# A fused retention and squared-ReLU kernel: the first weight block issued ahead of the first cast of v, fewer warm-up matmuls, and new written-out orders for every engine

## The chip, the cores and the metric

The kernel runs on one core of one Trainium2 chip. The metric is the device time of one execution in microseconds (us). The kernel before takes 283.64 us, the median of three runs (283.6, 283.64 and 287.75).

A core has five engines that run side by side, each through its own list of instructions in order: PE (matmuls; its weight loads are listed as PEld), DVE (vector), ACT (scalar), POOL (GpSimd) and SP (which here only issues DMA transfers). POOL issues transfers too: those that convert float32 to float16 on the way. The transfers themselves run on 16 DMA engines.

## The reference

With eight sequences, eight heads, 576 positions and head size 64, a retention layer feeds a two-layer network with a squared ReLU:

```python
scores = scale * np.matmul(q, k.transpose(0, 1, 3, 2))
rel = pos[:, None] - pos[None, :]
Dmat = np.where(rel >= 0, gamma[:, None, None] ** rel[None, :, :], 0.0)
ret = scores * Dmat[None, :, :, :]
attn_out = np.matmul(ret, v)
...
x = np.ascontiguousarray(attn_out.transpose(0, 2, 1, 3)).reshape(B * S, H * D)
h = x @ w_in
r = np.maximum(h, 0.0)
g = r * r
return g @ w_out
```

x has 4608 rows of 512, w_in is 512 x 2048 and w_out is 2048 x 512, all in float32. The kernel computes in float16 with float32 sums.

## The kernel before

**Tiling.** The positions are cut into 36 units of 128 rows: four full chunks for each of the eight sequences, and four "tail" units that hold the last 64 rows of two sequences each. Two units make a group; there are 18 groups. A group goes through two stages. The retention stage makes xT (the rows x, transposed) out of q, k and v and a running state R. The feed-forward stage multiplies xT with w_in, applies ReLU and square (gT), and multiplies gT with w_out.

**Retention.** The first eight units are loaded in pairs (add_load_pair, L441 and L444). Their k, q and v are cast on DVE, ACT and POOL to float16 (kx and qx at L555 and L553; vx, with a decay, at L548, one half on POOL and one half on DVE), transposed on PE (psT, L570) and copied out of PSUM as kqT (L587). Then come small matmuls, all issued by the helper quad at L483: psc (scores), psS (sums for the state), psO (outputs). DVE masks the scores (rx, L624), updates the state (stmp at L646, R at L597) and makes xT out of psO (L711). Later units are loaded one by one (L419, L422; tails L425), cast on POOL (kq at L497, L512, L508; v at L518) and transposed by DMA (kqT, L529); ACT copies their psO to xT (L887).

**Feed-forward.** The first product writes ph (L1207, or in seven-product Strassen form L1056), ACT and DVE take ReLU and square (L1217, L1224, L1226, L1085, L1099), and the second product writes po (L1246 for the first group, L1302 in Strassen form behind it). The sums that Strassen's form needs are made on DVE (stage, L1275; wT, L982; pair_c, L1020; xs, L1041). Results go to o (L1318, L1328, L1379, L1254) and are stored by SP (L999, and L1004 for the tails).

**Weights.** w_in and w_out come in eight blocks, numbered 0 to 7, each issued by POOL (L459) as a converting transfer. The first one is made to wait for the load of v of the first pair (the call of behind in add_weight). SP's load of k for the pair that starts at unit 4 waits for weight block 5 in the same way.

**The order of the work.** Nothing is scheduled while the program is built. A class Schedule holds 1848 tasks (1844 after the change) with their dependences; the list ORDER, written out by hand from a search, gives the one order in which all tasks of all engines are emitted, so it fixes the order on each engine. SLOTS gives, tag by tag, which buffer each tile takes: "ff" is the rotation of the eight PSUM banks. Tasks of the engine SP stand in ORDER with the rest, so SP's queue of loads, transposes and stores is fixed too. A store that waits for its tile holds up what is queued behind it on SP.

**Warm-ups and fillers.** WARM matmuls on zeros (L392) stand in the lead-in, before PE has real work. Empty PE instructions ("fillers") are set in two ways. FRONT of them are dealt out behind the warm-ups, some per warm-up. PADS gives, for each long run of small matmuls, how many are spread over the larger matmuls ahead of that run. They change at which instruction each run begins.

Of the kernel before, what the change touches and what calls it, by code (L numbers as in the profile page):

```python
# [73 lines left out]

SLOTS = {
    "ff": (
        "012345671235467210354216503216504123250356270617026170243671023026307156423105305315031472632140160724075325461034607134"
        "572614356746243562751420753140517345151076245010176145026157032173652056417016752657421360274072301673461053045206106214"
        "754067342671274302567325642076217067065460215722452361726434230"),
    "kq16": "012345610624530164204563014253601245306124503162",  # L80
# [1369 lines left out]
```

## Time and profile before

| what | us |
|---|---|
| median of three runs | 283.64 |
| own time of the profiled execution | 285.19 |
| span of the profiled execution, first to last instruction | 283.3 |
| PE busy | 273.1 |
| DVE busy | 202.5 |
| ACT busy | 197.2 |
| POOL busy | 100.7 |

The profile comes from one execution. Its own time is 1.9 us more than its span, which leaves out what lies before the first and behind the last instruction. Matmuls are pipelined, so that a busy PE is not a PE at its peak. The granted clock of PE is 1.000 over the whole span.

A row of the timeline gives start, duration, engine, line, operation, the tiles written and read, shapes and count; in brackets stands how long the engine was idle before it and what ended that wait. A row of the table of waits gives who waited for what, the sum in us, the number of times, and the longest. A row of the chain gives start, duration and what ran; the chain is followed backwards from the last instruction to whatever released each step. A row of the table by stretches gives the stretch, its length, each engine's busy time, the clock, the busy share of the DMA engines and their GB/s.

### The profile page before, as it was taken

The page shows a single profiled execution, that of the slowest core. Times are in us where ns is not written, and L with a number is a line of the kernel's source. Part 1 is how long each engine was busy: PE and PEld are TensorE (multiplying, and loading weights), DVE is VectorE, ACT ScalarE, POOL GpSimd, SP SyncE. Part 2 cuts the span into 40 slices and gives each one's busy share as a digit, 9 for nine tenths or more (in the row PEclk, how much of TensorE's full clock was granted, in tenths as well). Part 3 has the DMA queues.
Part 4 walks back from the last instruction along what each step waited for, and adds up shares of the span by engine and source line. Part 5 has one row for each costly group of instructions (what it writes and reads, how often), then busy time and mean ns, then how long its engine had stood idle before and what let it go on. Part 6 is the DMA issues. An engine that isn't in the chain of part 4 may idle for free.

```text
span 283.3 us, 11597 instructions
## 1 busy us (share of the span) xinstructions
PE 273.1 (96%) x4730; PEld 236.8 (84%) x4730; DVE 202.5 (71%) x405; ACT 197.2 (70%) x374; POOL 100.7 (36%) x133
## 2 busy tenths in 40 slices
PE   8799999999999999999999999999999989999994
PEld 3477677888899889989998998899879878999883
DVE  4781588989788958567887877767786866574562
ACT  6647786576759865996779568767688665787931
POOL 7650034714533743516256124444454230000000
PEclk9999999999999999999999999999999999999999
DMA  6999998889599999989799798897979890104014
GB/s 207 277 206 207 246 325 198 182 207 203 135 188 206 226 214 183 203 188 190 172 213 209 148 194 186 189 186 198 174 179 217 211 139 5 39 1 187 2 74 148
DMA packets 119154, 50.03 MB, mean 177 GB/s; under 512 B 94784, under 2 KB 113728, under 8 KB 119104
## 3 DMA queue, kind: packets, MB, share of 16 engines
q1 hardware_dynamic: 114560, 44.84, 73.4%
q0 software_dynamic: 4224, 4.19, 9.1%
q8 instruction: 39, 0.64, 1.0%
q10 hardware_dynamic: 320, 0.26, 0.4%
q14 instruction: 11, 0.09, 0.1%
HBM read 36.70 MB, written 9.44 MB: 163 GB/s over the span
## 4 chain that ended last, share of the span: by engine, by line
PE 78%; DMA 11%; ACT 2%; SPq 2%; POOL 2%; DVE 1%; issue 1%; POOLq 0%; DVEq 0%
PE po L1302 33%; PE ph L1207 22%; PE ph L1056 16%; PE psO L483 4%; DMA w_in<-in_moe_w_in_dram 4%; DMA loads<-in_v_dram 2%; DMA pair_c<-in_v_dram 2%; DMA loads<-in_q_dram 2%; DMA kqT<-kq 1%; SPq L425 1%; PE psS L483 1%; PE psc L483 1%; ACT gT L1224 1%; POOL vx L548 1%; SPq L441 1%
## 5 line engine op out<-in xcount | busy, mean ns | idle before, releaser
L1207 PE MATMUL ph<-xT,w_in 128*128 128x256 f16 x640 | 84.0, 273 | 1.2 <-issue 0.6
L1207 PEld LDWEIGHTS <-w_in 128*128 128x128 f16 x640 | 61.4, 98 | 11.3 <-issue 1.5
L1217 ACT ACTIVATE gT<-ph 128x512 f16<-128x512 f32 x80 | 46.1, 599 | 18.6 <-PE ph L1207 18.5
L1302 PEld LDWEIGHTS <-gT 128*128 128x128 f16 x544 | 51.0, 98 | 6.8 <-issue 0.4
L1302 PE MATMUL po<-w_out,gT 128*128 128x256 f16 x272 | 45.8, 273 | 0.0
L1302 PE MATMUL po<-wT,stage 128*128 128x256 f16 x272 | 42.3, 273 | 0.6 <-ACT xT L887 0.6
L1302 PEld LDWEIGHTS <-stage 128*128 128x128 f16 x408 | 38.2, 98 | 5.5 <-issue 0.6
L1302 PE MATMUL po<-wT,gT 128*128 128x256 f16 x272 | 41.4, 273 | 0.0
L1224 ACT ACTIVATE gT<-gT 128x512 f16<-128x512 f16 x66 | 40.2, 636 | 0.2
L512 POOL TENSOR_TENSOR kq<-loads,qexp 128x512 f16<-128x512 f32 x24 | 25.5, 1062 | 32.2 <-DMA loads<-in_q_dram 32.2
L497 POOL CAST kq<-loads 128x512 f16<-128x512 f32 x28 | 18.4, 656 | 50.4 <-DMA loads<-in_k_dram 50.3
L1056 PEld LDWEIGHTS <-pair_c 128*128 128x128 f16 x512 | 32.8, 98 | 1.2
L1099 ACT ACTIVATE gT<-gT 128x1024 f16<-128x1024 f16 x32 | 33.3, 1058 | 0.7 <-DVE gT L1085 0.5
L1275 DVE TENSOR_TENSOR stage<-gT,stage 128x512 f16<-128x512 f16 (+1 forms) x51 | 31.2, 622 | 3.0 <-ACT gT L1224 2.8
L518 POOL TENSOR_TENSOR v<-loads,vdec_full 128x512 f16<-128x512 f32 x24 | 28.8, 1208 | 9.1 <-DMA loads<-in_v_dram 9.1
L1085 DVE CUSTOM_DVE_ANT_0 gT<-ph,parts 128x512 f16<-128x512 f32 x24 | 16.5, 688 | 13.7 <-PE ph L1056 8.4
L1056 PEld LDWEIGHTS <-w_in 128*128 128x128 f16 x384 | 24.9, 98 | 0.9
L1318 ACT COPY u<-po 128x256 f32<-128x256 f32 x34 | 12.8, 376 | 17.8 <-PE po L1302 17.8
L887 ACT CAST xT<-psO 128x512 f16<-128x512 f32 x28 | 16.0, 589 | 10.1 <-PE psO L483 10.1
L1085 DVE CUSTOM_DVE_ANT_0 gT<-ph,stage 128x512 f16<-128x512 f32 x24 | 16.4, 685 | 7.4 <-PE ph L1056 7.3
L1066 ACT COPY parts<-ph 128x512 f32<-128x512 f32 x24 | 14.1, 587 | 10.6 <-PE ph L1056 10.3
L1328 DVE TENSOR_TENSOR o<-po,u 128x256 f32<-128x256 f32 x33 | 13.8, 419 | 10.5 <-ACT u L1318 5.2
(111 smaller groups left out, 433.3 us busy)
## 6 DMA issues: line engine op xcount, KB each, us to landing
out_dram<-o SPq DMA_DIRECT2D x32, 256.0 KB, 3.6
loads<-in_k_dram SPq DMA_DIRECT2D x24, 256.0 KB, 4.3
loads<-in_q_dram SPq DMA_DIRECT2D x96, 64.0 KB, 3.3
loads<-in_v_dram SPq DMA_DIRECT2D x24, 256.0 KB, 3.8
w_in<-in_moe_w_in_dram POOLq DMA_DIRECT2D x4, 512.0 KB, 8.8
w_out<-in_moe_w_out_dram POOLq DMA_DIRECT2D x4, 512.0 KB, 14.4
pair_c<-in_k_dram SPq DMA_DIRECT2D x2, 512.0 KB
pair_c<-in_q_dram SPq DMA_DIRECT2D x4, 256.0 KB, 5.9
```

The lines of the kernel that those rows point to most:

```text
L483: t = nc.tensor.matmul(out_, lhsT=lhsT, rhs=rhs, start=start, stop=True, skip_group_check=True, tile_position=(64 * row, 64 * col))
L497: op(out=out_.rearrange("p (n b a d) -> p n b a d", n=2, b=2, a=2), in_=in_.rearrange("p (a n b) d -> p n b a d", n=2, a=2))
L512: nc.gpsimd.tensor_tensor(out=out_.rearrange("p (t a d) -> p a t d", t=4, a=2), in0=tile_of["q32", u].rearrange("p (a t) d -> p a t d", a= ...
L518: nc.gpsimd.tensor_tensor(out=t, in0=tile_of["v32", u], in1=vdec[kind].rearrange("p (h o) -> p h o", o=1).to_broadcast([P, H, D]), op=ALU. ...
L1056: nc.tensor.matmul(out_[:, e], lhsT=left[:, m, fi * P:(fi + 1) * P], rhs=right()[:, m], start=fresh and e == 0 and m == 0, stop=m == HK - ...
L1085: nc.vector._custom_dve(TENSOR_ADD_SAT, out=g_at(s, h, j), in0=bank(j, x), in1=part_at[name].rearrange("p (e t) -> p e t", t=P), s0=3.4028 ...
L1099: nc.scalar.activation(out=t, in_=t, func=ACTF.Square)
L1207: nc.tensor.matmul(tile_of["ph", g, fb][:, j, :], lhsT=w_in16[:, m, fi * P:(fi + 1) * P], rhs=tile_of["x", g][:, m, :], start=(m == 0), st ...
L1217: nc.scalar.activation(out=tile_of["g", g][:, nf * fb:nf * (fb + 1), :], in_=tile_of["ph", g, fb], func=ACTF.Relu)
L1224: nc.scalar.activation(out=t, in_=t, func=ACTF.Square)
L1275: (nc.gpsimd if eng == "POOL" else nc.vector).tensor_tensor(out=S_(k)(sl), in0=in0(sl), in1=in1(sl), op=op)
L1302: nc.tensor.matmul(tile_of["pb", g, bank], lhsT=left(i), rhs=right[:, i, :], start=(start and i == 0), stop=(i == HF - 1), skip_group_chec ...
```

## The change

The task list changes in three places, and then everything that was searched over it is new. The first cast of v of the first pair (the half on POOL) is made to depend on the issue of the first weight block, so that on POOL the issue comes first. WARM goes from 34 to 30. FRONT goes from 56 to 64, and up to three fillers, not two, follow each warm-up. Five numbers of PADS change, from 553 in all to 549. ORDER and SLOTS are other lists. All other code is the same; lines behind L561 move down by two.

```diff
 ORDER = """
-0 34 1 2 3 35 4 5 6 36 7 8 9 70 10 71 11 37 12 13 72 76 73 14 38 77 15 16 75 74 78 17 79 18 39 19 80 81 40 20 319 82 314 320 83 21 41 22 315 23 42 24
...
+0 30 1 2 3 4 5 6 31 7 8 9 10 66 11 32 12 13 67 72 14 15 74 68 16 33 17 69 73 18 75 19 20 76 77 21 36 22 34 23 71 24 310 70 25 35 78 26 311 27 28 79 38
...
@@ SLOTS
-    "kqT": "012340123041203140213041203140213041",
+    "kqT": "012341023410234012304120314021304120",
...
@@ emit
-                for i in range(min(self.front, 2)):
+                for i in range(min(self.front, 3)):
                     self.filler()
-                self.front -= min(self.front, 2)
+                self.front -= min(self.front, 3)
...
-    PADS = (41, 0, 0, 4, 86, 0, 0, 0, 12, 140, 84, 141, 45, 0, 0, 0, 0, 0, 0, 0, 0, 0, 0, 0, 0, 0, 0, 0, 0, 0)
-    FRONT = 56
+    PADS = (41, 0, 0, 4, 86, 0, 0, 0, 11, 130, 82, 147, 48, 0, 0, 0, 0, 0, 0, 0, 0, 0, 0, 0, 0, 0, 0, 0, 0, 0)
+    FRONT = 64
...
-    WARM = 34
+    WARM = 30
...
             if xs[name][0]["eng"] == xs[name][1]["eng"]:
                 sched.need(xs[name][1], xs[name][0])
+            if name == "v" and lead:
+                sched.need(xs[name][0], issues[0])
```

What the new lists do, engine by engine, where the steps of the prediction touch it:

- POOL: before, vx of the first pair, weight blocks 0, 1 and 2, vx of the second pair, block 3, and blocks 4 to 7. After: block 0, vx of the first pair, blocks 1 and 2, vx of the second pair, block 3, blocks 4 to 7.
- DVE in the lead-in: before, vx of the first pair, kqT copy, R, rx, stmp, three rx, vx of the second pair, R, two xT. After: kqT copy, vx of the first pair, three rx, R, rx, stmp, R, vx of the second pair, two xT.
- PE in the lead-in: before, 14 warm-ups, psT of k, 4 warm-ups, psT of q, 3 warm-ups, psS, psc, 6 warm-ups, psT, 3 warm-ups, psT, 4 warm-ups, psO, psS, psc, then 32 matmuls of ph. After: 14 warm-ups, psT of k, 5 warm-ups, psT of q, 6 warm-ups, psc, 4 warm-ups, psS, psT, 1 warm-up, psT, psO, psc, psS, then 32 matmuls of ph.
- SP at the end: before, the loads of k and q of the last tail unit stand behind four output stores that are interleaved with the loads of the tail units before, and both last transposes stand together behind all loads. After: the load of q has two output stores (the two halves of one tile) fewer ahead of it. Behind it come the transpose of the other tail unit, those two stores, the two loads of v, and the last transpose.

PE has four matmuls and four weight loads fewer and four empty instructions more, out of some 10,080. DVE, ACT, POOL and SP have the same instructions in another order.

More of the change, by code (lines that the diff above doesn't have):

```diff
@@ L76 @@
     "ff": (
[L77 to L80, printed above, removed]
-    "kqT": "012340123041203140213041203140213041",
+        "012345671234057612340527460152764312560216750360537604537160457145670314576032632062625376142356721725314024570536175036"
+        "542106341545246154231406321746273416762704516727452410750427635407365276104520746712507634620654523507341526314265164513"
+        "023674053460316437251472456314016034125461540257325214031207620"),
+    "kq16": "012345610623450163251460124350612345016234501263",
+    "kqT": "012341023410234012304120314021304120",
     "R": "0123020201230120",
@@ L84 @@
     "gT": "012012012012012012",
-    "p1": "010101010101010100",
-    "o": "012345103012504102352504153045045132",
+    "o": "012345013142012405130324032504041350",
+    "p1": "010101010101010101",
     "u2": "01010101010101010",
     "u4": "01010101010101010",
-    "v16": "0123401230413021403120413021",
+    "v16": "0123401230412031402130412031",
     "rT": "01010101010101",
```

108 rows, old and new, of the table ORDER are left out of this document.

## The prediction

> **What bounds the kernel now.** I read the page's busy table first, then its chain, then the table of waits on PE, then the timeline of the first 30 us and of the two places behind them where PE waits longest.
>
> ```profile
> span 283.3 us, 11597 instructions
> PE 273.1 (96%) x4730; PEld 236.8 (84%) x4730; DVE 202.5 (71%) x405; ACT 197.2 (70%) x374; POOL 100.7 (36%) x133
> ...
> PE 78%; DMA 11%; ACT 2%; SPq 2%; POOL 2%; DVE 1%; issue 1%; POOLq 0%; DVEq 0%
> ```
>
> PE is busy for 273.1 of 283.3 us, and most of the chain that ends last is PE's own work. The change alters the order of that work, not its amount, apart from four warm-up matmuls. So it can win only what PE does not spend working: 283.3 - 273.1 = 10.2 us.
>
> ```profile
> PE psS L483 <- POOL vx L548: 1.5, 1, 1.5
> PE warm L392 <- DVE wT L255: 1.3, 1, 1.3
> PE psc L483 <- DMA kqT<-kq: 0.9, 1, 0.9
> PE ph L1207 <- issue: 0.6, 1, 0.6
> PE po L1302 <- ACT xT L887: 0.6, 1, 0.6
> PE ph L1207 <- DMA w_in<-in_moe_w_in_dram: 0.3, 1, 0.3
> PE psS L483 <- DVE vx L548: 0.2, 1, 0.2
> PE ph L1207 <- DVE xT L711: 0.2, 1, 0.2
> ```
>
> Every wait of PE is one place of its own (the middle number is the count). They sum to 5.6 us. The last matmul ends at 268.28 + 10.71 = 278.99 (row below), so another 283.3 - 279.0 = 4.3 us is the last store, whose order the change leaves as it was. The 1.3 us at the start wait for a memset that is not touched. What is open is therefore 5.6 - 1.3 = 4.3 us, of which 1.5 lies in the lead-in and 2.8 behind it.
>
> ```profile
> 2.69 5.98 DMA pair_c<-in_v_dram
> 8.84 1.52 POOL vx L548
> 10.36 1.62 POOL w_in L459 x2
> 11.98 10.16 DMA w_in<-in_moe_w_in_dram
> ...
> 24.57 3.23 PE ph L1207 x28
> ...
> 268.28 10.71 PE po L1302 x98
> ```
>
> This is the chain through the lead-in: the load of v, POOL's half cast of v (vx), POOL's issue of the weight blocks, their transfer, and the first product. From 24.57 on PE hardly stops. The chain thus names POOL's vx, 1.52 us, as what stands ahead of the weights, and that is what the change takes out of the way.
>
> **The change, part by part.** *The first weight block goes ahead of vx on POOL.*
>
> ```profile
> 8.77 0.69 DVE L548 TENSOR_TENSOR vx<-pair_c,vdec_pair 128x512 f16<-128x512 f32 x1 [0.98 <-DMA pair_c<-in_v_dram]
> 9.38 0.68 DVE L587 COPY kqT<-psT 128x512 f16<-128x512 f16 x1
> 10.30 2.42 POOL L459 DMA_DIRECT2D w_in<-in_moe_w_in_dram  x3
> 13.57 1.04 POOL L548 TENSOR_TENSOR vx<-stage,vdec_pair 128x512 f16<-128x512 f32 x1 [0.85 <-DVE rx L624]
> 13.97 1.18 DVE L548 TENSOR_TENSOR vx<-stage,vdec_pair 128x512 f16<-128x512 f32 x1
> 14.08 1.03 PE L392 MATMUL warm<-wT 128*128 128x512 f16 x4
> 15.04 0.64 PE L483 MATMUL psO<-rx,vx 64*64 64x128 f16 x32
> 15.08 0.41 DVE L597 TENSOR_TENSOR R<-stmp,dec 128x256 f16<-128x256 f32 x1
> 15.73 1.29 DVE L711 TENSOR_TENSOR xT<-psO,gam_full 128x512 f16<-128x512 f32 x2 [0.24 <-PE psO L483]
> 17.07 3.77 PE L1207 MATMUL ph<-xT,w_in 128*128 128x256 f16 x32 [0.18 <-DVE xT L711]
> 22.18 5.62 PE L1207 MATMUL ph<-xT,w_in 128*128 128x256 f16 x48 [0.25 <-DMA w_in<-in_moe_w_in_dram]
> 24.56 2.95 PEld L1207 LDWEIGHTS <-w_in 128*128 128x128 f16 x28 [0.31 <-DMA w_in<-in_moe_w_in_dram]
> ```
>
> The issue still waits for v's load, so it starts when vx did, 8.84 instead of 10.30, and takes 2.42/3 = 0.81. vx follows at 9.65 and ends between 10.69 (1.04, the other POOL vx) and 11.17 (its own 1.52). The second and third issues stay where they were, at about 11. Queued behind vx is psS, which PE reached at 10.41 and would now reach at up to 11.2; but PE's new order does psc first, and on DVE the kqT copy that psc needs now stands ahead of DVE's vx, so psc can start some 0.7 us (that vx's 0.69) sooner. The 0.8 us that vx loses is covered by psc (32 matmuls) and the four warm-ups put between; without that cover it would cost up to 0.8.
>
> What the weights win is bounded by 1.46 (the whole advance, 10.30 - 8.84) and by nothing, if the DMA engines were full anyway.
>
> ```profile
> 10.00:12.00 2.00, 1.59 (x68) 1.14 (x68) 1.15 (x4) 1.19 (x3) 2.00 (x4) 1.00 1.09 322
> 12.00:14.00 2.00, 2.00 (x22) 1.30 (x20) 2.00 (x5) 1.90 (x4) 1.15 (x2) 1.00 1.13 172
> 14.00:16.00 2.00, 1.92 (x55) 1.10 (x54) 1.76 (x4) 1.34 (x3) 2.00 (x3) 1.00 1.24 204
> 22.00:26.00 4.00, 3.79 (x34) 3.17 (x34) 1.29 (x2) 2.73 (x6) 0.00 (x0) 1.00 1.24 206
> ```
>
> The last two columns are the engines' busy share and GB/s. They were full before the weights came (1.09 of a nominal 1, at 322 GB/s with the loads of q, k, v) and after (1.24, at 204 to 206 with the casting weight loads). Only the seam, 12 to 14, runs below both rates: 172. Against 204 that is (204 - 172) x 2 us / 204 = 0.31 us of transfer, the nearest row to what can be won, so I take 0.3, nearer the lower end. It counts at 24.57, where the fourth block is the last that PE waits for (0.31 there and 0.25 at 22.18, so PE has the room to use it).
>
> PE must also be early. On DVE the decay R (15.08) now runs ahead of vx of the second pair, and the warm-ups that stood right before psO (14.08 to 15.11) are gone. R ended at 15.08 + 0.41 = 15.49; ahead of that vx it ends 1.18 sooner, at 14.3. vx of the second pair (1.18) and xT (1.29) follow, psO beside them, and ph starts near 16.8 instead of 17.07. That 0.3 is what the weights allow too, so PE can use the one and the other, and the two are not added.
>
> *Four warm-ups fewer, fillers elsewhere changed.* 4 of 34 matmuls whose group took 1.03 for four: 0.9 us of PE time, all inside stretches where PE otherwise waits for loads. Nothing by itself: the cover is the wait for v and q. The empty instructions are re-dealt (four fewer in the runs, eight more in the lead-in); PE's only wait that I can set beside them is the 0.6 "issue" in the table. Bounds 0.6 won to 0.6 lost; I take 0, as the change keeps the count of all PE instructions to within four.
>
> *The new orders, middle.* PE waits 0.6 for ACT's xT at 75.99, where a product needs the bank that the copy frees.
>
> ```profile
> 75.35 1.07 ACT L887 CAST xT<-psO 128x512 f16<-128x512 f32 x2 [1.59 <-PE psO L483]
> 75.99 0.38 PE L1302 MATMUL po<-wT,stage 128*128 128x256 f16 x2 [0.62 <-ACT xT L887]
> ```
>
> The rotation of banks and the order of products are new, so this place may vanish (0.6) or stay (0); I take half, 0.3.
>
> *The new orders, end.* PE waits 0.9 for the last transposes, which land at 233.5 (229.47 + 4.07).
>
> ```profile
> 222.15 1.31 SPq L425 DMA_DIRECT2D loads<-in_q_dram  x2
> 223.56 0.57 SPq L999 DMA_DIRECT2D out_dram<-o  x1
> 225.61 5.09 SPq L529 DMA_TRANSPOSE kqT<-kq  x2
> 228.26 1.18 POOL L508 TENSOR_TENSOR kq<-loads,qexp 128x256 f16<-128x256 f32 x2 [2.55 <-DMA loads<-in_q_dram]
> 229.47 4.07 DMA kqT<-kq
> ```
>
> SP's queue is a row of issues without a gap here; the q load issued at 222.15 lands for POOL at 228.26, and the transposed result follows only 5.3 us after that. In the new order two output stores fewer stand ahead of that load (2 x 0.57 = 1.1 us), and the first of the two transposes is no longer kept for the end. The two stores come right behind instead, with two loads of v, ahead of the last transpose; they fit in the 2.55 us in which POOL waits. Up to 0.9 to be had, 0 if the load is slower than its issue; I take 0.7.
>
> *New waits.* A new order of all engines makes places of its own. Between 0 and as much as PE shows now behind 30 us (0.9 + 0.6 + 0.6 + 0.2 = 2.3); I take 0.5, nearer the lower end, as PE shows only four such places in the 250 us behind the lead-in now.
>
> Sum: -0.3 - 0.3 - 0.7 + 0.5 = -0.8. The profiled execution's own time is 285.19 for its span of 283.3; it lies 1.55 above the median of 283.64. Against its own time the sum gives 284.4, against the median 282.8.
>
> **The rivals.** *The waits only move.* The same work, the same full SP and DMA queues: 0.3 of the seam is lost among the loads, and what goes at 76 and 233 comes back elsewhere (new waits 1.3 instead of 0.5). 283.64 - 0.3 - 0.3 - 0.7 + 1.3 = 283.6. For it: SP issues without a gap, so a load won in one place is waited for in the next. Against: two of the three largest waits have a visible cause that the order touches.
>
> *The weights crowd out the load of v for the second pair (slower).* The first block is issued by 9.65, while that load lands only by 13.57 at the latest (POOL's vx). If the two queues shared the engines evenly, the remaining 3.9 us would become up to 7.8, and v would land at 17.5. DVE's vx (1.18) and xT (1.29) stand in that order, so ph would start at 20.0; from 17.07 to 24.57 PE needs 7.50 less the 0.25 and 0.31 of waits, so it passes the old 24.57 at 26.9 instead of 24.57, 2.3 later. With the other terms (-0.3 - 0.7 + 0.5) that is 283.64 + 1.8 = 285.4. It decides from the point at which v lands later than 14.6 (14.6 + 1.18 + 1.29 = 17.07). Against it: the load has over half of its way behind it at 9.65, and a first packet needs time after the issue. The Trainium skill (DMA: Bandwidth & Descriptors, Queues, rings and completion order) says that a DMA engine takes turns between the queues that hold work, a packet at a time; by that rule v is slowed as in this rival, and the sum is 285.4 rather than 282.8. The seam's 172 GB/s at share 1.13 agrees that two queues at once move less than either alone, but no row here shows how they split.
>
> *All goes well (faster).* Every wait in the table but the first two goes and none comes: 283.64 - 2.8 = 280.8. For it nothing but the room; against it that the "issue" wait has no cause in the order.
>
> **How the numbers follow.** Forecast 0.50, waits only move 0.20, v crowded out 0.15, all goes well 0.10; 0.05 is left for an order that starves PE for longer than any row here shows. The predicted time is the forecast's, 282.8. The range goes from 280.8 (all goes well) to 283.64 + 2.3 = 285.9 (no gain, new waits at their upper bound), which takes in 285.4; about 0.13 lies outside. 2% of 283.64 is 5.7 us, about what a measurement of this kernel can tell from no change (its three runs span 4.15). Faster than 278.0 would need more than the room, 4.3: 0.02. Slower than 289.3 needs the starving order: 0.04. Within 2%: 0.94.
>
> **What would show it.** In the new profile POOL's first w_in issue should start near 8.8 and its vx near 9.7; ph near 16.8 and the group that waits for the fourth block near 24.3 instead of 24.57; PE's table of waits should lack psS behind POOL's vx, and the waits for xT and kqT should be gone or below 0.3. If DVE's vx of the second pair starts after 14.6, the rival with v holds. If PE's waits behind 30 us still sum to 2.3 or more, the orders brought nothing, and a sum above 4 makes the prediction wrong.

## The result and the profile after

The changed kernel takes 282.98 us (median of 20 runs, 281.12 to 284.23) where the kernel before takes 285.06 us beside it (20 runs, 282.46 to 287.75). The ratio is 0.9947, with a 95% interval from 0.9922 to 0.9972: about 1.5 us (0.0053 x 285.06), too little for the bound of 2%, but not nothing. The medians are 2.1 us apart; the ratio leaves out the runs that are over 1.5% above the fastest of their kernel, three of the kernel before and none of the changed one. Two more measurements of the same two kernels gave 0.9932 (0.9906 to 0.9959) and 0.9959 (0.9930 to 0.9988).

The forecast said 282.8; it said so by a sum of -0.8 from 283.64, and 283.64 was the median of only three runs. That the time came out at 282.98 is luck: the starting point was 1.4 us too low and the gain was summed 0.7 (by the ratio) to 1.3 (by the medians) too small, and the two errors cancel. The terms of the sum are mostly not the ones that gave the gain.

The profiled execution after has 283.93 us of its own time. These are the page's lines that answer to those shown of before:

```profile
span 282.0 us, 11585 instructions
PE 273.1 (97%) x4726; PEld 237.5 (84%) x4726; DVE 198.0 (70%) x405; ACT 198.4 (70%) x374; POOL 100.9 (36%) x133
...
PE 63%; DMA 16%; SPq 10%; DVE 4%; POOL 2%; issue 2%; ACT 1%; POOLq 0%; DVEq 0%; ACTq 0%
```

PE's busy time is the same 273.1 us; the gain lies in what PE waits. The waits on PE after, as total, count and longest:

```profile
PE psc L483 <- DMA kqT<-kq: 1.3, 2, 0.9
...
PE ph L1209 <- DVE xT L713: 0.5, 2, 0.3
PE psc L483 <- ACT kqT L589: 0.5, 1, 0.5
PE ph L1209 <- DMA w_in<-in_moe_w_in_dram: 0.3, 1, 0.3
PE psS L483 <- issue: 0.2, 1, 0.2
PE po L1304 <- DVE o L1330: 0.2, 1, 0.2
PE psc L483 <- issue: 0.2, 1, 0.2
```

The waits for POOL's vx, for ACT's xT and the "issue" of 0.6 are gone. The largest entry is new: waits for a transposed kqT, now in the middle (0.37 at 112 us and 0.93 at 124) and not at the end. Behind 30 us the waits of the table sum to 1.9, where before they were 2.3. The lead-in after, from the timeline:

```profile
9.37 0.93 POOL L459 DMA_DIRECT2D w_in<-in_moe_w_in_dram  x1 [2.14 <-DMA pair_c<-in_v_dram]
10.37 1.36 POOL L548 TENSOR_TENSOR vx<-pair_c,vdec_pair 128x512 f16<-128x512 f32 x1
...
13.90 1.04 POOL L548 TENSOR_TENSOR vx<-stage,vdec_pair 128x512 f16<-128x512 f32 x1 [0.69 <-PE psT L572]
13.98 1.25 DVE L599 TENSOR_TENSOR R<-stmp,dec 128x256 f16<-128x256 f32 x1
15.15 0.68 DVE L548 TENSOR_TENSOR vx<-stage,vdec_pair 128x512 f16<-128x512 f32 x1
17.08 3.65 PE L1209 MATMUL ph<-xT,w_in 128*128 128x256 f16 x32 [0.34 <-DVE xT L713]
```

The block is issued ahead of vx, as the change says, but at 9.37 and not at the 8.84 at which vx started in its place. The first ph starts at 17.08, where before it was 17.07.

To see where 1.5 us come from I used the same sum on every profile of this study: the durations of PE's products at full pace, added in order (0.109 us for 256 columns, 0.056 for 128, 0.216 for 512, 0.012 and 0.023 for the quads of 64 and 128 columns), and subtracted from the time at which PE has come so far. The result is what PE has lost up to there. Both kernels do 261.9 us of such work. By stretches of that work, in us lost:

```
profile                      to 24   24-66  66-102 102-114 114-216 216-end   sum
  (time at the end, about)     37      80     117     129     232     278
before                       12.90    1.98    0.05   -0.09    1.19    1.32  17.36
before, again                12.80    1.55    1.34   -0.09    0.76    0.32  16.69
after                        12.66    0.61    0.36    1.00    1.32    0.29  16.26
after, again                 12.95    0.32    0.21    1.04    0.73    0.29  15.55
after, a third time          12.86    0.53   -0.18    1.11    0.79    0.29  15.40
old order, mean of 4         12.92    1.58    0.44    0.03    1.19    0.60  16.77
new order, mean of 8         12.79    0.46    0.10    1.18    1.51    0.29  16.34
```

The last two lines take in experiments whose edit is small or lies elsewhere (below): b_block0_first and b_new_pads in the old order, and a_block0_back, a_mid, a_end_back, a_end_back2 and a_old_pads in the new one. The unchanged kernels differ by 17.03 - 15.74 = 1.3 us on the mean, which is what the times say within their interval; the last two lines differ by 0.4 only. A single execution strays by more than the whole gain, so the table shows places better than it shows the sum. Two stretches stand out: from 37 to 80 us the new order wins 1.1 to 1.3 us (old 1.25 to 1.98, new 0.26 to 0.67, without overlap), and from 117 to 129 us it loses 1.1 (old -0.09 to 0.37, new 1.0 to 2.0 in seven profiles and 0.04 in the eighth). These two cancel. The rest of the difference between the unchanged kernels comes from two waits of the old order, 1.1 near 110 us and 0.9 near 233, each in one of the two profiles of before. The lead-in, where the one visible edit of code is, gives 0.1.

### The profile page after: what moved, and what is told of

It reads as the page before. It is cut to its first block, busy times and chain, and to the rows that moved or that the text cites. A ratio compares the mean times of both kernels' runs of the same rounds, so it can differ in the third digit from the quotient of the medians.

```text
span 282.0 us, 11585 instructions
## 1 busy us (share of the span) xinstructions
PE 273.1 (97%) x4726; PEld 237.5 (84%) x4726; DVE 198.0 (70%) x405; ACT 198.4 (70%) x374; POOL 100.9 (36%) x133
## 4 chain that ended last, share of the span: by engine, by line
PE 63%; DMA 16%; SPq 10%; DVE 4%; POOL 2%; issue 2%; ACT 1%; POOLq 0%; DVEq 0%; ACTq 0%
PE po L1304 28%; PE ph L1209 15%; PE ph L1058 13%; DMA w_out<-in_moe_w_out_dram 5%; SPq L419 5%; DMA loads<-in_q_dram 4%; PE psO L483 3%; DMA pair_c<-in_v_dram 3%; SPq L441 2%; DMA stage<-in_q_dram 2%; DMA kqT<-kq 2%; DMA out_dram<-o 2%; SPq L422 1%; SPq L529 1%; PE psS L483 1%
## 5 line engine op out<-in xcount | busy, mean ns | idle before, releaser
L1209 PE MATMUL ph<-xT,w_in 128*128 128x256 f16 x640 | 83.0, 273 | 0.9 <-DVE xT L713 0.5
L1304 PE MATMUL po<-w_out,gT 128*128 128x256 f16 x272 | 44.8, 273 | 0.0
L1304 PE MATMUL po<-wT,gT 128*128 128x256 f16 x272 | 40.8, 273 | 0.2 <-DVE o L1330 0.2
L497 POOL CAST kq<-loads 128x512 f16<-128x512 f32 x28 | 19.2, 687 | 54.0 <-DMA loads<-in_k_dram 49.6
L512 POOL TENSOR_TENSOR kq<-loads,qexp 128x512 f16<-128x512 f32 x24 | 26.8, 1116 | 22.1 <-DMA loads<-in_q_dram 21.8
L518 POOL TENSOR_TENSOR v<-loads,vdec_full 128x512 f16<-128x512 f32 x24 | 27.4, 1146 | 10.7 <-DMA loads<-in_v_dram 10.6
L1277 DVE TENSOR_TENSOR stage<-gT,stage 128x512 f16<-128x512 f16 (+1 forms) x51 | 27.9, 561 | 0.8
L1304 PE MATMUL po<-w_out,stage 128*128 128x256 f16 x136 | 21.2, 273 | 0.0
```

The source lines that it names most:

```text
L497: op(out=out_.rearrange("p (n b a d) -> p n b a d", n=2, b=2, a=2), in_=in_.rearrange("p (a n b) d -> p n b a d", n=2, a=2))
L512: nc.gpsimd.tensor_tensor(out=out_.rearrange("p (t a d) -> p a t d", t=4, a=2), in0=tile_of["q32", u].rearrange("p (a t) d -> p a t d", a= ...
L518: nc.gpsimd.tensor_tensor(out=t, in0=tile_of["v32", u], in1=vdec[kind].rearrange("p (h o) -> p h o", o=1).to_broadcast([P, H, D]), op=ALU. ...
L1209: nc.tensor.matmul(tile_of["ph", g, fb][:, j, :], lhsT=w_in16[:, m, fi * P:(fi + 1) * P], rhs=tile_of["x", g][:, m, :], start=(m == 0), st ...
L1277: (nc.gpsimd if eng == "POOL" else nc.vector).tensor_tensor(out=S_(k)(sl), in0=in0(sl), in1=in1(sl), op=op)
L1304: nc.tensor.matmul(tile_of["pb", g, bank], lhsT=left(i), rhs=right[:, i, :], start=(start and i == 0), stop=(i == HF - 1), skip_group_chec ...
```

## The experiments

All ratios are to the kernel before, run on the same chip beside each. Three sets share a chip each: the two kernels once more with both block-0 experiments; b_two_mended, a_mid, a_end_back and a_no_fillers; and a_end_back2, a_old_pads, b_new_pads and r_after2. So the changed kernel itself stands beside the experiments of the first and the third set, not of the second. Each of the twelve was profiled once.

**The two kernels once more.** No edit.

> The kernel before, unchanged, profiled once more: it tells which of PE's waits come back at the same place and which belong to one execution. Theory (single places set the gain): PE waits again near 76 us for ACT's xT (0.6), near 233 us for the last transposed kqT (0.9) and in the lead-in for POOL's vx (1.5), each within 0.3 of that. Rival (chance of the execution): at least two of the three are gone or changed by more than half. Ratio to the kernel before 1.000 within 0.003 by either.

> The changed kernel, unchanged, profiled once more. Theory: no wait over 0.3 us near 76 and near 233, the wait near 124 us for a transposed kqT again about 1 us, the first weight block issued ahead of vx, the fourth block's group near 24 us; ratio 0.993 to 0.998. Rival: the places and sizes of the waits differ as much between two executions of this kernel as between the two kernels, and the ratio is nearer 1.000.

Measured: before again 284.84 us, ratio 1.0027 (0.9994 to 1.0060); after again 282.81, ratio 0.9932 (0.9906 to 0.9959). The first is one kernel against itself, so it also tells how far a ratio strays. Two of the three places of before came back (xT 0.6, vx 1.8 in two places), the one near 233 did not; PE waits 1.1 near 110 for DVE, which the first profile of before does not have. After shows the wait near 124 again (1.0) and none near 76 and 233. So the place at 76 and the one at 124 belong to the orders, and the wait at 233, which carried the largest term of my sum, to one execution.

**The block-0 edit, undone and alone.**

```diff
 changed kernel, ORDER and code (a_block0_back)
-77 21 36 22 34 23 71 24 310 70 25
+77 21 22 34 23 71 24 310 70 36 25
-            if name == "v" and lead:
-                sched.need(xs[name][0], issues[0])
 kernel before, ORDER (b_block0_first)
-75 74 78 17 79 18 39 19 80 81 40 20
+75 40 74 78 17 79 18 39 19 80 81 20
```

> The changed kernel with the issue of the first weight block put back behind POOL's half cast of v; all else, the new orders too, as changed. Theory: the block is issued about 1.3 us later, the seam of 12 to 14 us falls from about 240 GB/s towards 170 to 200, the first four blocks land up to 0.5 later, and the time goes up by 0.2 to 0.4 us (ratio to the changed kernel 1.001). Rival (the edit brings nothing, the orders all): landing of blocks 1 to 3 within 0.2 of the changed kernel's and the same time. Rival (the early block crowds out v of the second pair): with the block back, that load lands 0.3 or more earlier and the time falls by 0.3 or more.

> The kernel before with one edit: the first weight block is issued ahead of POOL's half cast of v; the orders of PE, DVE, ACT and SP stay those of before. Theory: issue near 8.8 and vx near 9.7; psS, which stands next on PE here, waits up to 0.8 longer for vx, hidden by PE's wait for the weights; the blocks land 0.3 to 0.5 earlier, and the time falls by 0.3 (ratio 0.999). Rival (no cover without the new orders): the late vx pushes psS, psO and the first ph by 0.8, so that the first ph starts near 17.8 and the time rises by up to 0.5. Rival (crowding): v of the second pair lands over 0.3 later than in the kernel before, POOL's and DVE's vx of that pair move by as much.

Measured: undone, 282.72 us, ratio 0.9939 (0.9914 to 0.9965), beside 282.81 for the changed kernel on the same chip; alone, 285.05, ratio 1.0022 (0.9993 to 1.0052). Neither shows a gain by the edit. In b_block0_first, where PE's old order stands, the late vx does cost something, as the expectation's first rival said: psS waits 1.9 us for it (1.5 before), and the first ph starts 0.9 later than the 17.07 of before.

```profile
PE psS L483 <- POOL vx L548: 1.9, 1, 1.9
...
17.96 3.67 PE L1207 MATMUL ph<-xT,w_in 128*128 128x256 f16 x32
```

POOL's timeline with the block back in the changed kernel:

```profile
8.71 1.04 POOL L548 TENSOR_TENSOR vx<-pair_c,vdec_pair 128x512 f16<-128x512 f32 x1 [1.25 <-ACT kqT L589]
9.70 2.42 POOL L459 DMA_DIRECT2D w_in<-in_moe_w_in_dram  x3
13.52 1.04 POOL L548 TENSOR_TENSOR vx<-stage,vdec_pair 128x512 f16<-128x512 f32 x1 [1.41 <-DMA stage<-in_v_dram]
```

The seam, as the window of 12 to 14 us (the last columns are clock, DMA share and GB/s), in the changed kernel:

```profile
12.00:14.00 2.00, 1.88 (x61) 1.27 (x53) 1.97 (x6) 1.69 (x4) 1.31 (x3) 1.00 1.24 242
```

with the block back:

```profile
12.00:14.00 2.00, 2.00 (x78) 1.73 (x81) 2.00 (x5) 1.89 (x4) 0.59 (x2) 1.00 1.24 228
```

and in the kernel before, second profile:

```profile
12.00:14.00 2.00, 2.00 (x23) 1.41 (x22) 2.00 (x5) 1.86 (x4) 1.11 (x2) 1.00 1.18 211
```

Three things took the gain away.

First, the seam filled and nothing came of it. In the nine profiles in which the first block goes out by 9.70 (b_block0_first and the new order with its block back are among them) the window reads 221 to 242 GB/s; in the five in which it goes out at 10.19 or later it reads 172 to 211. But the block lands no earlier: at 16.22 to 17.06 in seven profiles of the new order with the block first, at 16.34 to 17.00 in four of the old order and at 16.67 with the block put back. The fourth block, for which PE was to wait, lands at 24.0 to 25.0, at 24.4 to 25.5 and at 24.3. (In b_block0_first they land at 16.04 and 24.26, a little earlier, but there PE is late.) The signs of the theory did not come: with the block back the seam stays at 228.

Second, vx is shorter in the new order: POOL's took 1.52 where DVE's vx of the same load ran beside it (8.77 and 8.84 in the profile of before), and takes 1.04 here, where DVE's comes at 10.33. So with the block behind vx it goes out at 9.70 already, and not at 10.30.

Third, the block put first doesn't start when vx would. In seven profiles of the new order with the block first (all but a_no_fillers, where it is 10.19) it starts between 9.00 and 9.64, while vx in its place starts at 8.71 to 8.84 in five profiles. The block's earliest start, from the timeline of a_old_pads:

```profile
9.00 0.93 POOL L459 DMA_DIRECT2D w_in<-in_moe_w_in_dram  x1 [1.78 <-ACT kqT L589]
```

and the latest, from the third profile of the changed kernel:

```profile
9.64 0.93 POOL L459 DMA_DIRECT2D w_in<-in_moe_w_in_dram  x1 [2.44 <-ACT kqT L589]
```

The advance by the edit is thus 9.70 - 9.29 (the mean of the seven) = 0.4 us, and by the whole change 0.9 to 1.0 (10.19 to 10.30 in four profiles of the old order), not 1.46. The names in brackets, a copy on ACT mostly, mislead here: the landing of v in the trace tells what holds the issue. The issue starts 0.30 us behind that landing in the eight profiles with the block first that show the landing, vx 0.16 to 0.17 behind it in the five others. The larger part is that v itself lands later, at 8.70 to 9.34 in those eight against 8.54 to 8.67 in these five, though its load is issued at 2.7 in all. Why it lands later no run shows.

**The two places of PE's order.** Into the kernel before I put what the new order does at 41 and at 74 us, and nothing else; the row of banks of SLOTS is permuted to match.

```diff
 ORDER
-103 582 592 346 531 586 118 543 106 602 585 544 104 603
+103 582 592 531 586 118 543 106 602 585 544 104 603 346
-154 723 722 696 724 482 374 155
+154 722 696 482 374 723 724 155
```

> The kernel before with two places of its PE order mended and nothing else of the change: four tasks of products are put between psT and the psS that waits for vx at 41 us, and eight ph matmuls are put behind the quad run at 74 us, ahead of the po that waits for ACT's xT because it takes psO's bank. Theory (the gain of the change is these two places: 0.4 to 0.5 at 41 and 0.6 to 0.7 at 74.7 in all three profiles with the order of before, nothing in the three with the new one): both waits go, nothing comes in their place, and the time falls by 1.0 us, ratio 0.9965. Rival (the waits only move): PE arrives earlier, meets the next late operand, and the time stays within 0.3 of the kernel before. Rival (the gain is the block-0 edit): the same, no gain.

The places themselves, first in the kernel before (second profile), then in the changed kernel (second profile):

```profile
40.58 0.61 PE L570 MATMUL psT<-ident,qx 128*128 128x128 f16 x8
41.53 0.45 PE L483 MATMUL psS<-vx,kx 64*64 64x64 f16 x32 [0.34 <-POOL vx L548]
...
75.46 0.38 PE L1302 MATMUL po<-wT,stage 128*128 128x256 f16 x2 [0.62 <-ACT xT L887]
```

```profile
40.95 0.61 PE L572 MATMUL psT<-ident,qx 128*128 128x128 f16 x8
41.39 0.38 PE L1304 MATMUL po<-w_out,gT 128*128 128x256 f16 x2
41.61 0.81 PE L1248 MATMUL po<-w_out,gT 128*128 128x512 f16 x3
42.35 0.44 PE L483 MATMUL psS<-vx,kx 64*64 64x64 f16 x32
...
74.20 0.23 PE L483 MATMUL psO<-kqT,Rm 64*64 64x64 f16 x4
74.36 1.27 PE L1304 MATMUL po<-wT,stage 128*128 128x256 f16 x10
```

In the old order psS stands right behind the transposes, and POOL's vx is 0.34 late for it; in the new one 0.96 us of products stand between. At 74 the old order's next product takes the bank that psO has just filled, so it waits until ACT has copied psO out; in the new order the next ten products use a bank that is free. With both mended in the old kernel:

```profile
41.70 0.61 PE L570 MATMUL psT<-ident,qx 128*128 128x128 f16 x8
42.14 0.38 PE L1246 MATMUL po<-w_out,gT 128*128 128x512 f16 x1
42.83 0.38 PE L1302 MATMUL po<-w_out,gT 128*128 128x256 f16 x2 [0.31 <-ACT kqT L587]
...
75.14 1.05 PE L1207 MATMUL ph<-xT,w_in 128*128 128x256 f16 x8
76.02 0.38 PE L1302 MATMUL po<-wT,stage 128*128 128x256 f16 x2
```

At 74 the wait is gone and nothing comes for it until 117 us: 1.05 us of ph cover the copy. At 41 the wait moved by one product: the po that I brought forward takes the bank of an earlier psT, which ACT still reads. From 37 to 80 us this profile loses 1.00, between old and new. Its time is 285.24, ratio 0.9996 (0.9956 to 1.0035); the interval holds the 1.0 us that I expected as well as nothing, and its profile has a lead-in that is 1.0 us later than the others of the old order (13.91). So the profile shows the place at 74; the time decides nothing, and no run shows that these two places carry the gain.

**The wait at 123 us.** I meant to take it away by moving a load behind two others.

```diff
 ORDER
-961 399 200 205 971 972 206 402
+961 399 205 971 972 206 200 402
 dma_task (allows another order of the loads; changes no instruction by itself)
-        t = add("SP", key, dur, fn, deps=list(last_load) + list(more), **kw)
+        t = add("SP", key, dur, fn, deps=list(more), **kw)
```

> The changed kernel with one load moved on SP: v of unit 20 goes behind k and q of unit 21, so that the transposed kqT of unit 21, for which PE waits 1.1 us at 123 us in two of three profiles with the new order, is issued earlier. Theory (that wait is a new one that the new order of SP makes): kqT is issued 0.5 to 1.3 us earlier, the wait falls below 0.5, and the time falls by 0.5 to 1.0 (ratio to the kernel before 0.990). Rival (the load stream as a whole is late in those executions, whatever its order): the wait stays at about 1 us, or v of unit 20 is waited for in its place, and the time stays.

Measured: 284.21 us, ratio 0.9964 (0.9932 to 0.9997); the wait is there, 1.38. But the experiment missed its place. Counted along SP's queue the transpose that PE waits for is that of unit 19, not 21, and the loads that I moved come behind it. It is one more profile of the wait and no test of its cause. What the traces show of the cause: in the changed kernel (second profile) and in the kernel before (second profile) the load of q of that unit, POOL's use of it and the transpose are, in this order,

```profile
111.84 2.43 SPq L419 DMA_DIRECT2D loads<-in_q_dram  x4
...
118.30 1.04 POOL L512 TENSOR_TENSOR kq<-loads,qexp 128x512 f16<-128x512 f32 x1 [1.81 <-DMA loads<-in_q_dram]
...
119.36 2.28 SPq L529 DMA_TRANSPOSE kqT<-kq  x1
...
124.05 0.32 PE L483 MATMUL psc<-kqT 64*64 64x64 f16 x16 [0.97 <-DMA kqT<-kq]
```

```profile
106.98 1.23 SPq L529 DMA_TRANSPOSE kqT<-kq  x1
...
109.77 2.11 SPq L419 DMA_DIRECT2D loads<-in_q_dram  x4
...
115.88 1.29 SPq L529 DMA_TRANSPOSE kqT<-kq  x1
```

Between these two profiles the load goes out 2.1 us and the transpose 3.5 us later in the new order. In it the load of q of the unit before stands behind a transpose (of unit 17) and not ahead of it. That this order is the cause is argued from the two queues, not tried.

But 115.88 is the earliest of the old order. In the first profile of before the same transpose goes out at 118.43, and PE does not wait for it:

```profile
118.43 1.29 SPq L529 DMA_TRANSPOSE kqT<-kq  x1
```

Over the four profiles of the old order in the table above it is issued at 117.3 on the mean, over the eight of the new one at 119.2. And PE comes to this place earlier in the new order: it starts the pair of psc there at 122.7 on the mean of the eight (121.9 to 123.4) against 124.2 on the mean of the four (123.3 to 125.0). So the wait is made of two shifts of like size, a transpose 1.8 us later and a PE 1.5 us earlier. In b_new_pads, the profile of the old order in which PE is earliest, a wait stands at the same place:

```profile
123.34 0.30 PE L483 MATMUL psc<-kqT 64*64 64x64 f16 x16
123.91 0.32 PE L483 MATMUL psc<-kqT 64*64 64x64 f16 x16 [0.27 <-DMA kqT<-kq]
```

One profile of the new order, that of a_block0_back, has the same order on SP and no wait: its transpose goes out at 117.81. So an execution whose loads run some 1.5 us earlier does without the wait.

**The end of SP's order, put back.**

```diff
 ORDER (1150: the two stores, 304: q, 302: the transpose, 305: v)
-... 304 ... 302 ... 1150 ... 305 ...
+... 1150 304 ... 305 302 ...
```

> The changed kernel with the end of SP's order put back: the two output stores go ahead of the last load of q, and the transpose of the other tail unit goes behind the last loads of v, next to the last transpose. Theory of the forecast (0.7 us come from there): the last transposes are issued 1 to 4 us later, PE waits 0.5 to 1 us for them near 233, and the time rises by 0.7. Rival (the wait at 233 belongs to executions in which the load stream is late; 1.0 in one profile of before and none in two others): no wait over 0.3 in this profile, and the median within 0.3 of the changed kernel, perhaps with a wider spread.

> The changed kernel with the end of SP's order put back, once more, now beside the changed kernel itself. Theory (the end of the order is worth something in executions whose load stream is late): 0.5 to 1.2 us slower than the changed kernel, with a wider spread. Rival (it is worth nothing, the first measurement differed by its chip): within 0.4 of it.

Measured: the first time 284.88 us, ratio 0.9984 (0.9950 to 1.0017), then 284.99, ratio 0.9972 (0.9946 to 0.9999), the second beside the changed kernel's 283.96, ratio 0.9959 (0.9930 to 0.9988). Both are on the slower side of the changed kernel, and their intervals overlap its own. In the first of the two the last two transposes do go out later, at 223.2 and 226.0 against 218.6 and 224.4 in the first profile of after, but neither profile shows a wait for them. The second has this at 224:

```profile
224.48 0.32 PE L483 MATMUL psc<-kqT 64*64 64x64 f16 x16 [0.45 <-DMA kqT<-kq]
```

but it waits there for a transpose that was issued at 219.31, ahead of all that I moved: the whole load stream was late in that execution (the same transpose goes out at 215.19 in the first profile of after). So this experiment settles little. The stretch behind 232 us lost 0.29 in every profile of the new order, with the end put back too, and 0.32 to 1.32 in those of the old one. What the new end is worth lies between nothing and the 1.0 us by which the medians of the second comparison differ (0.4 by its ratios), and no wait in a profile stands for it.

**The empty instructions.** Once all taken out of the changed kernel, once only their five new numbers exchanged, both ways.

```diff
 a_no_fillers
-    PADS = (41, 0, 0, 4, 86, 0, 0, 0, 11, 130, 82, 147, 48, 0, ...)
-    FRONT = 64
+    PADS = (0, 0, 0, 0, 0, 0, 0, 0, 0, 0, 0, 0, 0, 0, ...)
+    FRONT = 0
 a_old_pads (b_new_pads is the reverse, in the kernel before)
-    PADS = (41, 0, 0, 4, 86, 0, 0, 0, 11, 130, 82, 147, 48, 0, ...)
+    PADS = (41, 0, 0, 4, 86, 0, 0, 0, 12, 140, 84, 141, 45, 0, ...)
```

> The changed kernel without any of its empty PE instructions (PADS all zero, FRONT 0). It tells what re-dealing them can have moved. Theory (the fillers shift only where instruction code is fetched, and the change's eight more in the lead-in are worth nothing): within 0.5 of the changed kernel either way. Rival (the fillers carry part of the gain): PE shows waits of the kind issue that the changed kernel lacks, and the time rises by 1 us or more.

> The changed kernel with the five numbers of PADS as they were, 553 empty instructions in the runs instead of 549. Theory (the count of empty instructions matters by microseconds, but these five numbers shift places behind 160 us by a few instructions only): within 0.4 of the changed kernel. Rival (the re-dealt fillers carry the gain): 0.8 us or more slower, and a wait of the kind issue of 0.5 or more behind 160 us in the profile.

> The kernel before with the five new numbers of PADS and nothing else. Theory: within 0.4 of the kernel before, waits at 41 and 74 us as before. Rival (the re-dealt fillers carry the gain): 0.8 us or more faster.

> The changed kernel, unchanged, once more, as the measure for the other three of this set. Both theories: ratio to the kernel before 0.993 to 0.996, as in the two measurements before; the lead-in ends as in the other profiles of the new order, and the place at 74 us shows no wait.

Measured: without fillers 285.66 us, ratio 1.0000 (0.9960 to 1.0039). With the old numbers 284.42, ratio 0.9968 (0.9939 to 0.9998), beside the changed kernel's 283.96. The kernel before with the new numbers 286.21, ratio 1.0008 (0.9975 to 1.0041). So the five numbers are worth nothing that shows. The fillers as a whole may be worth about as much as the whole change: without them the ratio is that of the kernel before. The changed kernel did not run on that chip; beside a_mid, which did and differs from it by one load, the medians are 1.45 us apart, and the two intervals overlap. Without the fillers PE's table of waits has "issue" entries larger than in any other profile, where the longest is 0.7 (the profiled execution is the longest of its twelve, so these are at the upper end):

```profile
PE psS L483 <- issue: 1.6, 1, 1.6
PE ph L1058 <- issue: 1.3, 2, 0.9
```

"issue" is PE ready, with every operand there, and nothing arriving. The expectation's theory put the time within 0.5 us of the changed kernel; by the comparison with a_mid that was too small, and the waits that its rival named are there.

## Why the prediction was right in its time and half wrong in its terms

- *First block ahead of vx, -0.3.* The order on POOL came as said, the gain did not: undone, the edit costs nothing, and alone it brings nothing. The step that failed is the one from a fuller seam to earlier weights. The seam filled as forecast, from 172 to 242 GB/s in the two first profiles, but the first block lands at 16.2 to 17.1 us and the fourth at 24.0 to 25.5 in either order. I also let the issue start at 8.84, where vx had started; it starts at 9.3. The lead-in as a whole won 0.1 on the mean.
- *First ph near 16.8 by the earlier R.* Only in part: it starts at 17.08 in the first profile of after, and on the mean at 16.9 in eight profiles of the new order against 17.0 in the four of the old order with the block behind vx. I moved vx of the second pair, 1.18, as if its length belonged to it. Of that, 0.50 came from POOL's vx running beside it, and in the new order R (1.25 in the first profile of after, 0.41 before) or DVE's vx (1.55 in the second, 0.68 alone) is stretched by POOL's vx instead; the last section has the rows.
- *Cover for the late vx.* Held: psS waits at most 0.3 for POOL's vx in the profiles of the new order, though vx starts 1.5 us later than before (10.37 against 8.84). With PE's old order it does not hold: in b_block0_first the first ph is 0.9 late.
- *Wait for xT at 76, -0.3.* The mechanism was right, the size too small: it went wholly, from 0.6 in each profile of the old order to nothing in each of the new. I took half because the page did not tell whether the new order would keep it; but SLOTS and ORDER, read together, tell which bank the next product takes, and would have decided it.
- *The last transposes, -0.7.* Too much: 0.9 in the profile that I had, at most 0.2 in the three others of the old order. On the mean 0.3.
- *New waits, +0.5.* Too little: the wait at 123 alone costs 1.1.
- *What was left out.* The place at 41 us, where the table had only 0.2 for DVE's vx: psS waits for the later of two engines, and the whole stop is 0.3 to 0.5 in three of the four profiles of the old order. The new order puts products in between. (The 2.8 us that the prediction puts behind the lead-in hold 0.5, the waits of ph at 17.07 and 22.18, that lie in it; the 2.3 of its paragraph on new waits is right.)
- *Fillers, 0.* Held for the five numbers of PADS. The eight more in the lead-in were not tried alone.

Sum by the table, unchanged kernels only: 0.0 (lead-in) - 1.3 (37 to 80) - 0.6 (80 to 117, one wait of 1.1 in one profile of before) + 1.1 (117 to 129) + 0.0 - 0.5 (end) = -1.3, against -0.8 forecast. The two terms that recur in every profile or nearly so, -1.3 and +1.1, almost cancel; the two that make up the rest, -0.6 and -0.5, come from one profile of before each. So why the changed kernel is 1.2 to 1.9 us faster in three measurements is shown only in part, and no experiment that put a part of the change into the kernel before made it faster (1.0022, 0.9996 and 1.0008).

The rival in which the waits only move has half its say: the wait at 123 gives back most of what 41 and 76 bring, in good part because PE comes there 1.5 us earlier. The rival in which the weights crowd out the load of v had a sign that appeared without its cause: DVE's vx of the second pair starts at 15.15, behind 14.6, but right behind R (13.98 + 1.25), and POOL's vx of the same load was already free to start at 13.90. With the block put back, POOL's vx starts at 13.52, released by the load. The load itself takes 5.77 to 6.02 us from issue to landing in the five profiles with the early block that show its landing, and 5.93 in the second profile of before: it lost nothing that shows, and the first ph started at 17.08, not 20.0. The rival's sum counted too much from the start. In the kernel before the blocks were already issued at 10.30, some 3 us ahead of the landing of v, so whatever sharing there is was in the old time too. And the load is issued at 7.3 to 7.6 there, so that at 9.65 about a third of its time was behind it, not over half. The rule of the Trainium skill that was quoted for this rival (DMA: Bandwidth & Descriptors, Queues, rings and completion order), turns between queues packet by packet, is neither shown nor refuted: no run here shows the turns themselves. "All goes well" failed by the wait at 123.

Open stays why the times of before spread more (5.3 us over its 20 runs, 3.1 after). The profiles suggest that late executions of the load stream meet PE in more places in the old order, but no profile was taken of one of its long runs.

## What to carry to other kernels

Profile a finely ordered kernel more than once before a wait is priced: here the wait of 0.9 near the end belonged to one execution, and the one of 0.6 at 76 was in every one. A wait that goes can come back elsewhere, as PE then meets the next operand earlier; here that is half of the wait at 123. Where the order is a list with the banks written beside it, look up for each large wait whether the next product takes the bank or operand just being made; that tells from the code whether a wait belongs to the order. And before an instruction is moved ahead, ask what else sets its start: here 1.0 of the 1.46 us were not there to be won.

## What the runs showed that was not expected

The "issue" stops go with the supply of PE's own instructions. The trace has a DMA queue of instructions that brings 16 KB at a time, 39 packets over the span, some 6 us apart, and 37 without the 613 fillers of the changed kernel. The fourteen profiles have thirteen "issue" stops of PE over 0.15 us, and every one ends 1.2 to 1.5 us after such a packet has arrived; a stop at a random time would do that about once in twenty. Profiles with fillers have two of them at most, the longest 0.73; the one without fillers has five, together 3.5 us, the longest 1.61. So the "issue" wait of 0.6, which the prediction could set beside nothing, is very likely a wait for code. How the fillers help against it is not shown. The Trainium skill (Runtime: NRT & Kernel Launch, Instruction fetch mechanics) says that crossing from one block of fetched instructions to the next is mostly hidden; the trace agrees for most of the packets, and not for these thirteen.

POOL's half cast of v takes 1.52 us with DVE's half beside it and 1.04 without, as the rows above show; so an order on DVE set the duration of an instruction on POOL. It goes the other way too, when POOL's starts first; from the second profile of the changed kernel:

```profile
13.99 1.04 POOL L548 TENSOR_TENSOR vx<-stage,vdec_pair 128x512 f16<-128x512 f32 x1 [1.07 <-PE psT L572]
14.02 1.55 DVE L548 TENSOR_TENSOR vx<-stage,vdec_pair 128x512 f16<-128x512 f32 x1
```

DVE's takes 0.68 alone. Wherever POOL's vx overlaps in the first 17 us with DVE's vx or R, in all fourteen profiles, the one that starts later becomes longer by the time that they overlap, less some 0.13: 0.48 for 0.61 in the profile of before, 0.32 for 0.46 in that of after, 0.87 for 1.00 in the two rows above. Ahead of the place at 41 us the two start 0.05 apart, and which is first changes from one execution of before to the other; that decides for which engine psS waits there. The Trainium skill (SBUF — State Buffer, Who interferes with whom) says that a DVE instruction with two inputs in SBUF contends with a GpSimd one that reads SBUF, over ports that only one of them holds at a time, and that the order of issue decides who waits. The rows agree.

Two executions of one kernel differ by 4.5 us in when its last transpose is issued (229.5 and 225.0 in the two profiles of before), while their own times differ by 0.7 (285.19 and 284.48).
